# A new written-out instruction order for a linear-attention and MLP-mixer kernel on one core

## The chip, the cores and the metric

The kernel runs on one NeuronCore of a Trainium2 chip. The core has five engines with a queue of instructions each: TensorE (PE, matrix products), VectorE (DVE), ScalarE (ACT), GpSimd (POOL) and SyncE (SP, which here only issues transfers). Each takes its instructions in the order in which the program gives them, and waits at an instruction until what it needs is there. Sixteen DMA engines move data; transfers are issued from SP's or from ACT's queue. The metric is device time in microseconds (us), as the median of several runs.

## The reference

Inputs are q, k, v and alpha of shape (4, 8, 768, 48), that is batch, heads, time, head size, and four weight matrices. First a gated linear recurrence, for every batch and head:

```python
for t in range(S):
    state = alpha[:, :, t, :, None] * state + np.einsum('bhd,bhe->bhde', k[:, :, t], v[:, :, t])
    y[:, :, t] = np.einsum('bhd,bhde->bhe', q[:, :, t], state)
```

Its output, with the heads put side by side, is x of shape (4, 768, 384). Then a mixer:

```python
xt = x.transpose(0, 2, 1)
h = np.maximum(xt @ w_tok1, 0.0) @ w_tok2
u = x + h.transpose(0, 2, 1)
h2 = np.maximum(u @ w_ch1, 0.0) @ w_ch2
return (u + h2).astype(np.float32)
```

w_tok1 is 768 x 256, w_tok2 256 x 768, w_ch1 384 x 1536, w_ch2 1536 x 384. All is float32; the kernel computes its products in bf16 with float32 sums.

## The kernel before

**Blocks.** The recurrence is done in blocks of 256 steps, all 8 heads of a batch at once: 12 blocks, numbered n = 0 to 11, three to a batch. Within a block the decay is split off: the running sum of log alpha gives factors E and IE = 1/E, and with keys times IE and queries times E the block is two ordinary matrix products under a causal mask, plus what the state carries over. A block's operations are named by what they do, with n at the end:

- ld_at, ld_kt, ld_qt, ld_vt (line 545): loads of alpha, k, q, v, 384 KB each, into one of 20 "in" buffers.
- ln, cumw (blocks 0 to 2) or P, ln1, lnP, r1, cum (later blocks): logs on ACT, a pair product P on DVE or POOL, and the running sum as a product on TensorE. E, IE, Et: exponentials on ACT.
- k0a, q0r, kk, kl, qq, ql (lines 645, 649, 653): scaling of keys and queries on DVE or POOL. vb (line 698 or 697): cast of v.
- trk, trq: transposes of keys and queries on TensorE, evk, evq their copies out of the PSUM banks (blocks 0 to 5). From block 6 on the transposes are transfers (dk, dq, line 677) and pq puts the query in order.
- G0_, G1_: the score products of the block's two halves; mask0_, mask1_ (line 720, DVE).
- K: the product of keys and values for the state; vs0_, vs1_, ka, kb, kc are copies that it needs; s, sa, sm bring the state on (DVE or POOL).
- ia, ib: the carried state times queries; y0_, y1_: scores times values, in the same bank; x0_, x1_: the copy of the result.

**Mixer, for each batch b.** t1_b_m_c (line 805): first token product, six steps c (two per block) for m = 0, 1, using the weight pieces wt10 and wt11. ht_b_m: its ReLU. t2_b_i (line 810): second token product, with wt20, wt21, for six row tiles i. u_b_i: the sum with x. up, ut (batches 0, 1) or ux (batches 2, 3, a transfer, line 681): transposes of u. c1_b_m_h (line 829): first channel product for twelve columns m and two halves h, with weight pieces wc10 to wc15 (piece m // 2); rt: its ReLU (ACT line 800 or DVE line 802). c2_b_i_p (line 834): second channel product for row tile i in four parts p, with wc20 to wc25. o_b_i: the sum with u; st_b_i: the store. The last tile (batch 3, i = 0) is cut into 320 columns (h0) and 64 (h1).

**Weights.** 16 pieces of 384 KB are loaded (ldw_, lines 561 to 569) into the same 20 "in" buffers and cast to bf16 on ACT, POOL or DVE (cw_), where they stay.

**What sets the order.** The operations are not emitted in loops: the text ORDER (from line 375) lists all 946 in the order in which they are emitted, each with a letter for its engine: t TensorE, s ACT, v DVE, g POOL, y SP. BUFS lists the buffer that each value takes. An engine's queue is thus the list with only its letter. A load waits until every reader of the buffer's former content is done, and loads on one queue wait in line behind it. Operations marked f (f3_trq0: three, f1_K0: one) are matmuls on zeros that compute nothing and keep TensorE busy; there are 25 such matmuls.

**The shared port.** DVE and POOL operations that only touch SBUF take turns:

```python
        e, last = self.port_turn, self.port_last
        if e:
            if last and last[0] != e:
                self.tc.add_manual_dep(i.ins, last[1].ins.name,
```

So each of them waits for the last one before it in ORDER that ran on the other of the two engines.

Of the kernel before, what the change touches and what calls it, by code (L numbers as in the profile page):

```python
# [892 lines left out]
```

## Time and profile before

| what | value |
|---|---|
| device time, median of 3 runs | 165.01 us (164.99 to 165.9) |
| span of the profiled execution | 163.8 us |
| TensorE busy | 154.4 us (94%) |
| DVE, ACT, POOL busy | 110.7, 101.8, 75.6 us |
| bytes moved | 34.46 MB, mean 210 GB/s |
| issues on SP: inputs and weights, stores, transposes | 52, 16, 16 |
| issues on ACT: inputs and weights, stores | 12, 9 |

The page gives for the profiled execution its span, from the first to the last instruction; its device time is not given apart, so the time that lies around the span is read as the median less the span, 165.0 - 163.8 = 1.2 us. A busy TensorE is not TensorE at its peak, since the ends of its matmuls are modelled. In the stretches, a row is start and end, then the length, the busy time of PE, PE's weight loads, DVE, ACT and POOL with counts, the granted clock of TensorE as a share of full speed, the share of the DMA engines and GB/s. In the order of time, a row is start, length, engine, line, operation, out<-in, shape and count; in brackets the idle time before it and what ended it. In the groups, a row ends with the busy time in all, the mean of one in ns, and the idle time before it.

### The profile page before, as it was taken

What the parts mean: (1) busy time and instruction counts of PE and PEld (TensorE: products, weight loads), DVE (VectorE), ACT (ScalarE), POOL (GpSimd) and SP (SyncE); (2) the same over time, 40 slices, a digit from 0 to 9 for tenths busy, and PEclk for the clock granted to TensorE, in tenths of its full rate; (3) what the DMA queues carried; (4) which work ended last, traced back from release to release, by engine and by line L of the source; (5) the groups of instructions that cost most, each with busy time, mean ns of one, the idle gap of its engine ahead of it and who ended that gap; (6) DMA issues with size and microseconds to landing.
All of it is one profiled execution on the core that took longest, in us unless ns stands there. A gap on an engine that the chain in (4) does not pass through costs nothing.

```text
span 163.8 us, 4061 instructions
## 1 busy us (share of the span) xinstructions
PE 154.4 (94%) x1598; PEld 98.4 (60%) x1598; DVE 110.7 (68%) x197; ACT 101.8 (62%) x188; POOL 75.6 (46%) x94
## 2 busy tenths in 40 slices
PE   7958889899999999999999999999999999999991
PEld 2534656576657666666667666665566566666660
DVE  4244999698799767967889989873591283524341
ACT  3798799998999786389977948465515101562000
POOL 4055489884942827299795384748700000000000
PEclk9987999999999999999999999999999999999999
DMA  5999999999999997996899999689012135220214
GB/s 129 323 319 268 267 343 340 348 341 331 326 372 338 298 299 209 283 310 156 229 254 204 224 127 240 137 216 255 11 48 100 48 71 134 83 100 13 111 71 142
DMA packets 76322, 34.46 MB, mean 210 GB/s; under 512 B 68112, under 2 KB 76304, under 8 KB 76304
## 3 DMA queue, kind: packets, MB, share of 16 engines
q1 hardware_dynamic: 64704, 27.73, 66.2%
q10 hardware_dynamic: 11600, 6.49, 13.1%
q8 instruction: 12, 0.20, 0.5%
q14 instruction: 6, 0.05, 0.1%
HBM read 25.17 MB, written 4.72 MB: 182 GB/s over the span
## 4 chain that ended last, share of the span: by engine, by line
PE 57%; DMA 11%; POOL 9%; DVE 6%; ACT 6%; SPq 5%; issue 3%; ACTq 0%; POOLq 0%
PE ps L834 22%; PE ps L829 21%; DMA in<-in_v_dram 6%; PE ps L604 5%; SPq L545 4%; PE ps L810 4%; DMA in<-in_q_dram 4%; POOL pkk L653 3%; PE ps L805 2%; DMA in<-in_alpha_dram 2%; POOL vb L698 2%; DVE pkk L653 1%; PE ps L821 1%; DVE rt L802 1%; POOL in L645 1%
## 5 line engine op out<-in xcount | busy, mean ns | idle before, releaser
L834 PE MATMUL ps<-wc,rt 128*128 128x384 bf16 (+2 forms) x300 | 54.7, 320 | 0.0
L829 PE MATMUL ps<-ut,wc 128*128 128x384 bf16 x288 | 51.7, 326 | 0.2
L800 ACT ACTIVATE rt<-ps 128x384 bf16<-128x384 f32 x55 | 25.3, 494 | 25.4 <-PE ps L829 23.8
L834 PEld LDWEIGHTS <-rt 128*128 128x128 bf16 x300 | 27.6, 98 | 16.6
L829 PEld LDWEIGHTS <-wc 128*128 128x128 bf16 x288 | 27.1, 98 | 17.3 <-issue 0.7
L802 DVE TENSOR_SCALAR rt<-ps 128x384 bf16<-128x384 f32 x41 | 21.6, 552 | 13.8 <-PE ps L829 13.6
L720 DVE TENSOR_TENSOR gtm<-ps,mk 128x1024 bf16<-128x1024 f32 x24 | 28.3, 1219 | 2.7 <-PE ps L604 2.5
L653 POOL TENSOR_TENSOR pkk<-in,IE 128x384 bf16<-128x384 f32 (+1 forms) x12 | 14.3, 1206 | 9.3 <-DVE pkq L653 5.7
L838 DVE TENSOR_TENSOR o<-ps,u 128x384 f32<-128x384 f32 (+2 forms) x25 | 13.3, 536 | 6.1 <-PE ps L834 6.0
L814 DVE TENSOR_TENSOR u<-ps,x 128x384 bf16<-128x384 f32 x24 | 12.3, 553 | 4.1 <-PE ps L810 4.1
L653 POOL TENSOR_TENSOR pkq<-in,E 128x384 bf16<-128x384 f32 (+1 forms) x8 | 11.2, 1410 | 5.8 <-ACT tpk L697 2.9
L697 ACT CAST x<-ps 128x384 bf16<-128x384 f32 x19 | 9.0, 481 | 7.6 <-PE ps L604 7.6
L697 ACT CAST vb<-in 64x384 bf16<-64x384 f32 (+1 forms) x18 | 11.8, 657 | 2.6 <-POOL vb L698 1.4
L698 POOL CAST vb<-in 64x384 bf16<-64x384 f32 (+1 forms) x17 | 9.5, 559 | 8.0 <-DMA in<-in_v_dram 3.7
L805 PE MATMUL ps<-x,wt 128*128 128x384 bf16 x48 | 11.4, 326 | 0.3 <-ACT x L697 0.3
L810 PE MATMUL ps<-ht,wt 128*128 128x384 bf16 x48 | 10.1, 326 | 0.7 <-ACT wt L697 0.7
L589 POOL TENSOR_TENSOR in<-in 128x384 f32<-128x384 f32 x9 | 9.0, 999 | 3.2 <-DMA in<-in_alpha_dram 2.2
L653 DVE TENSOR_TENSOR pkq<-in,E 128x384 bf16<-128x384 f32 (+1 forms) x9 | 6.0, 689 | 6.3 <-ACT E L637 4.0
L645 POOL TENSOR_TENSOR in<-in,in 128x384 f32<-128x384 f32 x7 | 7.0, 1002 | 5.7 <-DVE in L649 3.0
L604 PE MATMUL ps<-tpq,tpk 48*64 48x128 bf16 (+1 forms) x288 | 8.5, 221 | 1.1 <-DVE ss L762 0.6
L768 DVE TENSOR_TENSOR tmp<-ps,ss 128x384 f32<-128x384 f32 x12 | 6.7, 555 | 4.1 <-POOL ss L771 2.3
L604 PEld LDWEIGHTS <-gtm 128*128 128x128 bf16 x192 | 7.6, 96 | 2.2 <-issue 0.6
(93 smaller groups left out, 212.9 us busy)
## 6 DMA issues: line engine op xcount, KB each, us to landing
in<-in_alpha_dram SPq DMA_DIRECT2D x11, 384.0 KB, 5.9
in<-in_q_dram SPq DMA_DIRECT2D x10, 384.0 KB, 5.5
in<-in_moe_w_ch_dram SPq DMA_DIRECT2D x10, 384.0 KB, 7.4
in<-in_k_dram SPq DMA_DIRECT2D x9, 384.0 KB, 5.3
in<-in_v_dram SPq DMA_DIRECT2D x9, 384.0 KB, 5.3
out_dram<-o SPq DMA_DIRECT2D x14, 192.0 KB, 2.4
out_dram<-o ACTq DMA_DIRECT2D x9, 192.0 KB, 1.9
in<-in_moe_w_tok_dram SPq DMA_DIRECT2D x3, 384.0 KB, 5.5
```

Of the source, the lines that this page charges most:

```text
L604: return self.pe.matmul(out, lhsT=lhsT, rhs=rhs, start=start, stop=stop, skip_group_check=True)
L653: self.shared(self.eng[e].tensor_tensor(self.t(dst)[:, c : c + z, :, 0:D], self.t(src)[:, :, c : c + z, :].rearrange("p h s d -> p s h d") ...
L697: return self.act.copy(d, s)
L698: return self.shared(self.eng[e].tensor_copy(d, s))
L720: self.nc.vector.tensor_tensor(self.t(gtm)[:, hf, :, :], self.pair(gp).rearrange("p a (j t) -> p (a j) t", t=128), bass.AP(tensor=m.tensor ...
L800: self.act.activation(d, s, AF.Relu)
L802: self.nc.vector.tensor_scalar_max(d, s, 0.0)
L805: self.pe.matmul(self.bank(bank)[:, 0:HD], lhsT=self.wt1[:, kc, m * 128 : m * 128 + 128], rhs=self.t(x), start=(kc == 0), stop=(kc == NS - 1))
L810: self.pe.matmul(self.bank(bank)[:, 0:HD], lhsT=self.wt2[:, kc, i * 128 : i * 128 + 128], rhs=self.t(hts[kc]), start=(kc == 0), stop=(kc = ...
L829: self.pe.matmul(self.bank(bank)[:, 0:HD], lhsT=self.wc1[:, kc, mc * 128 : mc * 128 + 128], rhs=self.t(ut)[:, 3 * half : 3 * half + 3, kc, ...
L834: self.pe.matmul(self.bank(bank)[:, 0 : cz - ca], lhsT=self.t(rts[mc][0])[:, i * 128 : i * 128 + 128], rhs=self.wc2[:, mc, ca:cz], start=( ...
L838: self.nc.vector.tensor_tensor(self.t(o)[:, ca:cz], self.bank(bank)[:, 0 : cz - ca], self.t(u)[:, i % 3, ca:cz], ALU.add)
```

## The change

Only ORDER and BUFS differ. The same 946 operations are listed in another order, and some with another letter:

- All loads are issued by SP: twelve that ACT issued before (wt11, wc20, wc25, and loads of blocks 4, 5, 6, 8, 9 and 10) go to SP, 64 in all. Of the stores, 12 go from SP to ACT and 7 from ACT to SP. SP's list has 91 entries instead of 84.
- The first loads are those of batch 0's blocks 0 to 2 and at3, then the four pieces of the token weights (places 14 to 17 among the loads; before: 15, 19, 20, 21), then the channel weights mixed with blocks 3, 4 and 5. kt3, vt3, at4 and qt3, which came ahead of the last token weights, now come after.
- On TensorE, t2 of batch 0 now stands ahead of trk3, cum4, trq3, G_3, K3, ib3 and trk4; 16 instead of 13 fillers stand ahead of cumw0.
- Copies, scalings and ReLUs change engine: 39 from ACT to DVE, 27 from DVE to ACT, 22 from ACT to POOL, 16 from POOL to ACT, 16 from POOL to DVE, 15 from DVE to POOL.
- At the end, the 64-column piece of the last tile comes last instead of the 320-column piece.

```diff
 ORDER = """
-f3_trk0t f1_trq0t f3_trq0t f3_cumw1t f3_cumw0t ld_at0y ln0s ld_at1y ln1s ld_qt0y ld_kt0y ld_vt0y cumw0t E0s ql0v
-ld_at2y f1_K0t f3_K0t cumw1t qq0v trq0t ld_kt1y ld_vt1y IE0s IE1s evq0v ld_qt1y Et0s vb0s kk0g E1s ld_at3y kl0g trk0t
-ln2s Et1s evk0s K0t kk1g kl1g s0_0v cumw2t vb1s vs0_0s Et2s E2s IE2s ld_qt2y vs1_0g qq1v ql1v G0_0t sa1_0t ln13s
-f1_trq1t sm1_0v f3_trq1t G1_0t K1t P3g ld_kt2y ld_vt2y lnP3s trk1t trq1t sa0_1t evk1s evq1s ld_kt3y qq2g mask0_0v
-mask1_0v ldw_wt10y ld_vt3y sm0_1v y0_0t cum3t x0_0s ib0t sa1_1t ld_at4y ld_qt3y ql2v trq2t sm1_1v kl2v E3s IE3s kk2g
-vs0_1g ldw_wt11s y1_0t evq2v G0_1t ia1t kk3g f1_G11t ldw_wt20y ldw_wt21y mask0_1v k0a3g x1_0s G1_1t ld_kt4y vb2s trk2t
-mask1_1v ldw_wc10y ib1t K2t evk2s r13s sa0_2t sm0_2v G0_2t cw_wt10s mask0_2v kl3g ldw_wc11y vs1_1g vs0_2g vs1_2s ka3s
-vb3s f3_G12t G1_2t kb3s ldw_wc13y t1_0_1_0t y0_1t trk3t ld_at5y y1_1t cw_wt11g ib2t ia2t ln14s mask1_2v y0_2t x0_1v
-x0_2v x1_1s vs1_3s vs0_3s ld_qt4s ldw_wc12y kc3g t1_0_1_1t y1_2t t1_0_0_0t t1_0_1_2t P4g t1_0_0_1t t1_0_0_2t t1_0_0_3t
-t1_0_0_4t q0r3g x1_2v t1_0_0_5t t1_0_1_3t evk3v qq3g t1_0_1_4t ql3g lnP4s t1_0_1_5t k0a4g ht_0_0s cw_wt20s K3t ht_0_1v
-cum4t cw_wt21s t2_0_0t t2_0_1t IE4s s0_3v sa1_3v u_0_0v t2_0_2t kk4g ldw_wc15y trq3t u_0_1v u_0_2v t2_0_3t t2_0_5t
-kl4g E4s evq3s up_0_0t t2_0_4t u_0_3v cw_wc10s u_0_5v u_0_4v up_0_1t ut_0_1s ut_0_0v ld_vt4y G1_3t G0_3t up_0_2t ib3t
-mask0_3v mask1_3v trk4t ldw_wc14y c1_0_0_0t c1_0_1_0t cw_wc11g ut_0_2s c1_0_2_0t c1_0_3_1t r14s cw_wc13s ldw_wc21y
-c1_0_7_1t evk4s y1_3t y0_3t rt_0_1_0v q0r4v ka4v qq4v ql4g x0_3s x1_3v rt_0_0_0v rt_0_2_0v P5g cw_wc15g c1_0_7_0t
-c1_0_6_1t rt_0_7_0s rt_0_7_1s cw_wc12s rt_0_3_1s c1_0_0_1t ld_qt5y c1_0_6_0t trq4t c1_0_2_1t c1_0_4_1t ld_kt5y
-ldw_wc22y sm1_3g cw_wc14g vb4g lnP5s c1_0_10_1t evq4s ldw_wc20s rt_0_0_1s rt_0_6_0v rt_0_6_1v ld_vt5s rt_0_2_1s
-c1_0_11_1t c1_0_11_0t rt_0_10_1v cum5t rt_0_11_1v G0_4t G1_4t kb4s IE5s rt_0_4_1v cw_wc21g kc4g ln15s E5s c1_0_10_0t
-c1_0_3_0t r15s rt_0_10_0s c1_0_9_1t vs1_4g ldw_wc23y mask0_4v rt_0_9_1s rt_0_11_0s mask1_4v ldw_wc24y c1_0_8_0t
...
-st_3_2y c2_3_5_1t c2_3_4_1t c2_3_5_2t c2_3_3_1t c2_3_4_2t c2_3_5_3t c2_3_0h0_0t c2_3_4_3t c2_3_3_2t c2_3_0h1_3t o_3_1v
-st_3_1y o_3_5v o_3_4v c2_3_3_3t c2_3_0h0_1t st_3_5y st_3_4y o_3_0h1v st_3_0h1y o_3_3v c2_3_0h0_2t c2_3_0h0_3t o_3_0h0v
-st_3_0h0y st_3_3s
+ld_at0y ln0s f3_cumw1t f3_trq0t f1_K0t f3_trk0t ld_at1y ln1s f3_K0t f3_cumw0t cumw0t Et0s IE0s E0s cumw1t E1s Et1s
+f1_trq1t ld_kt0y kl0g IE1s kk0v trk0t evk0s ld_vt0y vb0g ld_qt0y ld_at2y ln2s f3_trq1t K0t f1_trq0t ql0v qq0v trq0t
+evq0s s0_0v sa1_0t cumw2t G1_0t IE2s ld_qt1y ql1v qq1v trq1t ld_kt1y kk1v mask1_0v sm1_0v kl1g trk1t evk1v ld_kt2y
+vs1_0s E2s ld_vt1y evq1s G0_0t mask0_0v ib0t y1_0t f1_G11t G1_1t mask1_1v vs0_0g vb1s K1t Et2s vs1_1s x1_0s kl2g
+sa0_1t sm0_1v G0_1t mask0_1v ia1t y0_0t x0_0s vs0_1s kk2g trk2t ib1t sa1_1t ld_qt2y qq2g ql2g trq2t evq2s sm1_1v
+ld_vt2y vb2g y0_1t x0_1s ld_at3y ln13s P3g lnP3s K2t sa0_2t f3_G12t evk2v G0_2t G1_2t ia2t vs0_2s sm0_2v ldw_wt10y
+cw_wt10v t1_0_1_0t y1_1t vs1_2g t1_0_0_0t t1_0_0_1t mask0_2v y0_2t t1_0_1_1t t1_0_1_2t ldw_wt11y cw_wt11g x1_1s
+t1_0_1_3t ib2t t1_0_0_2t mask1_2v y1_2t x0_2v t1_0_0_3t ldw_wt21y t1_0_0_4t t1_0_1_4t x1_2s t1_0_1_5t ht_0_1v
+t1_0_0_5t ht_0_0s cum3t E3s IE3s cw_wt21g r13s ldw_wt20y cw_wt20g t2_0_2t t2_0_0t u_0_2v ld_kt3y k0a3g kl3g t2_0_3t
+ldw_wc10y cw_wc10s u_0_0v t2_0_5t t2_0_1t t2_0_4t u_0_3v up_0_1t ut_0_1s u_0_1v up_0_0t kk3g ka3s trk3t u_0_4v u_0_5v
+up_0_2t ut_0_0v c1_0_1_0t ld_at4y P4g c1_0_0_0t kb3g ln14s lnP4s ldw_wc13y cum4t cw_wc13g c1_0_7_0t ldw_wc11y cw_wc11g
+ut_0_2s c1_0_6_1t c1_0_6_0t c1_0_2_0t rt_0_0_0s rt_0_1_0v ld_qt3y qq3v E4s q0r3v ql3v ld_vt3y evk3s ldw_wc14y
+c1_0_3_1t c1_0_3_0t c1_0_1_1t rt_0_6_1v IE4s trq3t vb3g r14s rt_0_6_0v rt_0_3_1s vs0_3g rt_0_7_0s rt_0_2_0s c1_0_7_1t
+ld_kt4y vs1_3s rt_0_3_0s cw_wc14v rt_0_1_1v rt_0_7_1v c1_0_2_1t rt_0_2_1v c1_0_8_0t rt_0_8_0v kc3g K3t c1_0_0_1t evq3s
+G0_3t ldw_wc15y s0_3v cw_wc15s G1_3t c1_0_8_1t rt_0_8_1s kk4g k0a4g kl4g kb4s sa1_3v ld_at5y P5g ld_qt4y qq4g
+c1_0_10_0t q0r4g c1_0_11_1t mask1_3v ib3t mask0_3v c1_0_11_0t y1_3t c1_0_9_0t y0_3t rt_0_0_1v trk4t ldw_wc12y
+rt_0_10_0s rt_0_11_1v lnP5s cum5t x0_3v rt_0_11_0s cw_wc12s c1_0_5_0t c1_0_4_1t ldw_wc21y ldw_wc20y ql4v trq4t evk4v
+c1_0_5_1t x1_3v rt_0_9_0s rt_0_4_1v ln15s cw_wc21s c1_0_4_0t rt_0_4_0v rt_0_5_0v c1_0_10_1t cw_wc20g c2_0_4_0t evq4s
+G1_4t rt_0_10_1s sm1_3g ldw_wc22y cw_wc22v rt_0_5_1s G0_4t mask0_4v ia4t c2_0_1_0t c2_0_4_1t c2_0_1_1t ld_vt4y
+ldw_wc24y vb4s vs0_4s E5s r15s ldw_wc23y cw_wc23s y0_4t x0_4s c2_0_0_0t c2_0_2_0t ka4v cw_wc24s ld_at6y ln16s mask1_4v
+kc4g vs1_4g K4t P6v c1_0_9_1t sa0_4v sm0_4v sa1_4v c2_0_0_1t lnP6s c2_0_2_1t rt_0_9_1s IE5s r16s c2_0_4_2t ld_qt5y
+q0r5v cum6t c2_0_1_2t ib4t c2_0_0_2t ld_kt5y qq5v trq5t k0a5v kk5v c2_0_2_2t ldw_wc25y cw_wc25v evq5s y1_4t x1_4s
+ld_vt5y vb5g trk5t evk5v c2_0_4_3t IE6s c2_0_1_3t o_0_1v ld_at7y E6s sm1_4g o_0_4v t1_1_1_0t t1_1_1_1t t1_1_1_2t ln17s
+G0_5t G1_5t ld_kt7y mask1_5v k0a7g c2_0_0_3t c2_0_2_3t mask0_5v vs1_5s c2_0_5_0t c2_0_5_1t P7g vs0_5s kc5s K5t sa0_5v
+sm0_5v c2_0_5_2t ia5t y0_5t c2_0_5_3t ib5t ld_vt6y y1_5t ld_kt6y k0a6v t1_1_0_0t t1_1_0_1t t1_1_1_3t t1_1_0_2t kk6v
+ld_at9y ld_qt6y o_0_0v t1_1_0_3t x0_5s x1_5s t1_1_1_4t t1_1_1_5t ht_1_1v ld_vt7y vb6g lnP7s t1_1_0_4t t1_1_0_5t
+ht_1_0s vs0_6g ld_at8y c2_0_3_0t o_0_5v cum7t E7s IE7s t2_1_3t u_1_3v t2_1_5t u_1_5v st_0_1s q0r6g t2_1_1t c2_0_3_1t
...
+c2_3_1_2t o_3_4v c2_3_2_1t c2_3_1_3t c2_3_3_1t c2_3_3_2t c2_3_3_3t o_3_3v st_3_3y o_3_1v st_3_1y st_3_4s c2_3_5_3t
+o_3_5v st_3_5s c2_3_2_2t c2_3_2_3t o_3_2v c2_3_0h0_1t c2_3_0h0_2t c2_3_0h0_3t c2_3_0h1_0t c2_3_0h1_1t c2_3_0h1_2t
+o_3_0h0v st_3_0h0s c2_3_0h1_3t o_3_0h1v st_3_0h1s st_3_2y
...
 """
 BUFS = """
-3 0 4 1 11 1 13 0 5 3 11 2 0 0 1 6 0 1 2 0 0 17 0 0 9 1 0 1 2 0 1 0 1 16 0 4 0 2 0 6 0 4 7 1 3 3 1 6 1 0 5 2 1 6 5 2 1
...
+9 0 1 0 4 3 18 1 6 1 1 2 0 6 13 0 1 0 1 4 2 1 0 1 0 2 0 1 0 5 1 12 0 0 2 7 0 14 15 0 4 1 6 1 0 4 2 2 3 2 0 6 0 7 1 19
...
 """
```

More of the change, by code (lines that the diff above doesn't have):

```diff
@@ new lines @@
+c1_1_11_0t K6t o_0_2v c1_1_2_0t c1_1_2_1t IE8s ln18s k0a8v qq7v r18s s0_6v sa1_6v rt_1_2_1v rt_1_2_0v c1_1_10_0t
+c1_1_3_1t rt_1_3_1v c1_1_1_1t rt_1_1_1s c1_1_6_0t c1_1_4_1t rt_1_4_1v P9g c1_1_5_0t lnP9s ld_vt8y ld_qt9y c1_1_7_1t
+kk8g rt_1_7_0v rt_1_10_0s c1_1_5_1t sm1_6g kb7s ka7s ld_qt8y c1_1_8_1t rt_1_6_0s cum9t rt_1_7_1s q0r9g vs1_7g
+rt_1_5_0s c1_1_8_0t vb8v rt_1_0_1v st_0_2y rt_1_8_0v kc7s c1_1_6_1t vs0_8g rt_1_8_1v c2_1_1_0t rt_1_6_1v IE9s
+rt_1_11_0s K7t c1_1_3_0t rt_1_3_0v q0r8g dq6y pq6s ld_kt9y c1_1_9_0t qq8g rt_1_5_1s dq7y sa0_7v sm0_7v c1_1_10_1t
@@ new lines @@
+ia10t qq11g u_2_2v u_2_0v ux_2_0y y0_9t o_1_5v G0_10t c2_1_2_3t mask0_10v ld_kt11y c1_2_7_1t IE11s c1_2_4_1t rt_2_4_1s
+o_1_0v x0_9v y0_10t c1_2_9_1t st_1_0y c1_2_11_1t c1_2_1_1t rt_2_1_1v x0_10v rt_2_7_1s c1_2_0_1t c1_2_6_0t o_1_2v
+st_1_2s c1_2_10_1t rt_2_11_1s k0a11g c1_2_8_0t kk11g c1_2_6_1t c1_2_2_1t t1_3_0_0t rt_2_2_1s rt_2_10_1v rt_2_8_0s
+rt_2_6_0v st_1_5y dq11y c1_2_5_1t rt_2_0_1v c1_2_1_0t rt_2_1_0s ld_vt11y st_1_1y c1_2_0_0t c1_2_3_1t rt_2_5_1v
+rt_2_9_1s K10t c1_2_3_0t dk11y rt_2_6_1s rt_2_3_0s c1_2_8_1t c1_2_10_0t t1_3_0_1t t1_3_0_2t rt_2_0_0s sa0_10v
```

71 lines of the change are left out of this document (26 added, 45 removed), and 20 rows, old and new, of the table BUFS.

## The prediction

> **What bounds the kernel now.** I read the page's slices first, then the stretches (start:end in us, busy time of each engine, granted clock, DMA share, GB/s), then TensorE's own order of time.
>
> ```profile
> span 163.8 us, 4061 instructions
> PE   7958889899999999999999999999999999999991
> 20.00:36.00 16.00, 14.37 (x215) 10.12 (x213) 14.66 (x23) 15.51 (x27) 14.09 (x17) 1.00 1.12 342
> 36.00:56.00 20.00, 19.86 (x207) 13.12 (x205) 17.23 (x29) 17.86 (x35) 10.95 (x15) 1.00 1.10 338
> 56.00:100.00 44.00, 44.00 (x515) 28.70 (x514) 36.93 (x62) 33.17 (x65) 30.38 (x31) 1.00 1.05 231
> 100.00:160.50 60.50, 60.15 (x504) 37.19 (x502) 31.32 (x56) 20.87 (x44) 11.80 (x14) 1.00 0.41 108
> ```
>
> From 36 to 160.5 us TensorE idles for 0.14 + 0.00 + 0.35 us in all. So the end is set by the moment from which TensorE is full, by the work still ahead of it then, and by new holes. The amount of work is the same in both orders (393 PE entries, 25 fillers). The question is only what happens before 36 us and whether holes open later.
>
> ```profile
> 1.06 4.51 PE L604 MATMUL ps<-zs 128*128 128x512 bf16 x13 [1.06 <-DVE zs L507]
> 5.41 0.65 PE L604 MATMUL ps<-la,u 128*128 128x384 bf16 x3
> 6.29 1.02 PE L604 MATMUL ps<-zs 128*128 128x512 bf16 x4
> 10.50 0.62 PE L666 MATMUL ps<-idn,pkk 128*128 128x128 bf16 x8 [1.71 <-POOL pkk L653]
> 29.40 0.33 PE L604 MATMUL ps<-vb,pkk 128*128 128x96 bf16 x4
> 29.57 0.33 PE L604 MATMUL ps<-vb,kt 128*128 128x96 bf16 x4
> 29.95 0.32 PE L604 MATMUL ps<-la,u 128*128 128x384 bf16 x1
> 31.05 1.15 PE L810 MATMUL ps<-ht,wt 128*128 128x384 bf16 x6 [0.67 <-ACT wt L697]
> 32.04 0.62 PE L666 MATMUL ps<-idn,pkq 128*128 128x128 bf16 x8
> 32.50 0.81 PE L810 MATMUL ps<-ht,wt 128*128 128x384 bf16 x4
> 34.24 0.62 PE L604 MATMUL ps<-tpq,tpk 48*128 48x128 bf16 x16
> 34.79 0.51 PE L821 MATMUL ps<-idn,u 128*128 128x128 bf16 x6
> 35.46 0.62 PE L666 MATMUL ps<-idn,pkk 128*128 128x128 bf16 x8
> 35.92 2.60 PE L829 MATMUL ps<-ut,wc 128*128 128x384 bf16 x15
> ```
>
> The second token product (t2) starts at 31.05, after 0.67 us of waiting for the cast of a token weight, the first channel product (c1) at 35.92. From there on TensorE is full.
>
> **The change, part by part.** *Loads.* When does the k-th load land? Three waits on a landing show it:
>
> ```profile
> 4.31 0.84 ACT L598 ACTIVATE la<-in 128x768 bf16<-128x768 f32 x1 [2.23 <-DMA in<-in_alpha_dram]
> 16.63 0.52 ACT L592 ACTIVATE lf<-in 128x384 f32<-128x384 f32 x1 [0.44 <-DMA in<-in_alpha_dram]
> 32.48 1.00 POOL L645 TENSOR_TENSOR in<-in,in 128x384 f32<-128x384 f32 x1 [0.50 <-DMA in<-in_k_dram]
> ```
>
> These are the 1st, 10th and 22nd load, so from the 10th on (32.48 - 16.63)/12 = 1.32 us each. In the new list wt20, the last of the token weights, is 17th, where before the last of them was 21st: an estimated 25.9. kt3 is 18th: 27.2.
>
> *The start of attention.* 16 fillers now stand ahead of cumw0 instead of 13, at 0.215 us (four from 6.29 to 7.15): cumw0 starts at 6.05, not 5.41. Then a chain, with these rows:
>
> ```profile
> L631 ACT ACTIVATE E<-ps 128x400 f32<-128x400 f32 x9 | 4.5, 504 | 0.1
> L637 ACT ACTIVATE IE<-ps 128x768 f32<-128x768 f32 x3 | 2.4, 811 | 0.2 <-PE ps L604 0.2
> 12.08 1.95 POOL L653 TENSOR_TENSOR pkk<-in,IE 128x384 bf16<-128x384 f32 x2 [1.63 <-DMA in<-in_k_dram]
> L698 POOL CAST wc<-in 128x768 bf16<-128x768 f32 x6 | 5.0, 825 | 0.2
> 7.31 1.03 DVE L653 TENSOR_TENSOR pkq<-in,E 128x384 bf16<-128x384 f32 x2 [3.97 <-ACT E L637]
> 19.12 1.31 ACT L697 COPY tpq<-ps 128x1024 bf16<-128x1024 bf16 x1
> 16.03 2.35 DVE L720 TENSOR_TENSOR gtm<-ps,mk 128x1024 bf16<-128x1024 f32 x2
> 18.30 0.55 DVE L762 TENSOR_TENSOR ss<-ps,E 128x384 bf16<-128x384 f32 x1
> 28.00 0.69 DVE L698 COPY tpk<-ps 128x1024 bf16<-128x1024 bf16 x1
> ```
>
> cumw0 takes 0.9 (5.41 to 6.29), IE0 0.8 after a short Et0: 8.15. DVE and POOL take turns at their shared port in the written order, so kl0 (POOL 1.0), kk0 (DVE 0.55), vb0 (POOL 0.83) and ql0, qq0 (DVE 1.03) add up, then trq0 0.5, evq0 1.3, G1_0 0.35 and handoffs of about 0.4: the first mask starts at 14.1. From it to x0_2 DVE does six masks at 1.13, four state products at 0.47, two key copies at 0.69, one weight cast at 0.55, one x at 0.5: 11.1 us. With 0.7 for waits between x0_2 is done at 25.9. x1_2, the last t1, ht and IE3 follow on ACT and PE (0.5 each): IE3 at 28.2.
>
> The clock can lengthen this:
>
> ```profile
> 11.00:12.00 1.00, 1.00 (x20) 0.74 (x18) 0.02 (x1) 1.00 (x3) 0.00 (x0) 0.51 1.17 325
> 13.00:14.00 1.00, 1.00 (x19) 0.72 (x18) 0.00 (x0) 0.79 (x1) 1.00 (x2) 0.50 1.04 285
> ```
>
> Before, TensorE idled from 8.8 to 10.5 (the 1.71 above) and then had half its clock from 11 to about 14. The new order has holes of 1.1 and 0.7 us at 7.8 and 9.1 (waiting for E0, then kk0), so both are possible. At half clock trk0, three fillers, K0, trq0 and cumw2 cost 1.1 us more: IE3 28.2 to 29.4. [...]
>
> *t2 and c1.* t2 can start at about 27.4 (wt20 landed and cast, ht done). New is that trk3, whose input is made by three POOL products k0a3, kl3, kk3 of 1.0 us, stands on TensorE ahead of the first c1. k0a3 starts with kt3 at 27.2, kl3 with IE3 at 28.2 to 29.4, kk3 ends at 30.3 to 31.4, trk3 (0.46) and one up (0.34) follow: c1 at 31.2 to 32.3; I take 31.8, 4.1 us earlier than before.
>
> Against it stands work that before did ahead of c1 and the new order leaves for later: K3 0.34 (29.40 to 29.57, twice), cum4 0.29, trq3 0.46 (32.04 to 32.50), G0_3 and G1_3 0.55 (34.24 to 34.79), ib3 0.17 (four like K3's), trk4 0.46 (35.46 to 35.92). Sum 2.27. What is left is 1.8 us.
>
> *New waits after c1.* c1_0_7_0 needs the cast of wc13, which on POOL stands behind kk3, P4 (1.0) and kb3 (0.5): 30.85 + 1.0 + 0.5 + 0.83 = 33.2, and TensorE is there at 31.8 + 0.98 (two c1, six matmuls at 0.163) + 0.29 (cum4) = 33.07: 0.2 with the handoff. wc13's load must also wait until wt20's cast frees their common buffer; its issue at 27.4 and a landing 4 to 4.7 us later come before POOL is free. c1_0_9_1 gets its bank from x0_4, now behind the cast of wc23 on ACT: 0.45. pq9 moved from POOL to ACT behind x1_8, 0.2 ahead of G1_9. Together 0.9; bounds 0 and 1.5. Of the first c2 (wc20, 32nd load, 45.7 by the pace, cast 46.5; TensorE comes there at about 46.9) nothing is charged.
>
> *What costs nothing.* Twelve loads go from ACT's queue to SP's.
>
> ```profile
> 26.88 0.39 ACTq L545 DMA_DIRECT2D in<-in_q_dram  x1
> 26.87 0.51 ACT L697 COPY kt<-pkk 64x384 bf16<-64x384 bf16 x1
> 67.76 4.14 SPq L677 DMA_TRANSPOSE tpk<-pkk  x1
> 160.52 0.49 DVE L838 TENSOR_TENSOR o<-ps,u 128x320 f32<-128x320 f32 x1 [0.66 <-PE ps L834]
> ```
>
> An issue on ACT lay beside its compute, so ACT gains nothing. On SP the later ones (kt8, vt8, vt9, kt10) now stand behind transposes that hold SP for up to 4.14 us. By the same walk kk8 is wanted on POOL at about 74 us and vb8 at 78, some 8 us after those issues: covered; without the cover a wait there goes straight into K8 on TensorE. The evictions and scalings that change engines (ACT to DVE 39, DVE to ACT 27, and so on) lie under a full TensorE after 36 us; DVE there has 2.8 of 20 us free, ACT 2.1. They are priced only where named above.
>
> *The end.* The last add is over 64 columns instead of 320 (0.49), but the 320-column one now ends just before it: between 0 and 0.3, I take 0.2, nearer the row that stays.
>
> Sum: 4.1 - 2.27 - 0.9 + 0.2 = 1.1 us earlier. The execution profiled has a span of 163.8; the times shown have a median of 165.01, 1.2 above it, which I take as unchanged: 165.0 - 1.1 = **163.9**.
>
> **The rivals.**
>
> *TensorE is never held after t2* (the POOL chain is ready in time). t2 at 27.4, then t2 2.0 (twelve matmuls at 0.163), up 1.0 (three at 0.34, 34.79 to 35.13 as one stands there), trk3 0.46: c1 at 30.9; 5.0 - 2.27 + 0.2 gives 162.1. For it: POOL is idle for 1.9 of the 16 us here. Against it: kk3 alone needs 3 us after kt3.
>
> *One queue delivers more slowly, and the channel weights come late.* This ends slower.
>
> ```profile
> 3.00:12.00 9.00, 7.29 (x72) 4.19 (x71) 2.68 (x7) 6.80 (x11) 1.96 (x2) 0.95 1.16 322
> 12.00:20.00 8.00, 6.77 (x93) 4.31 (x92) 5.74 (x10) 6.30 (x10) 4.45 (x5) 0.85 1.01 266
> ```
>
> With loads from SP alone the rate was 322 GB/s, then 266; with both queues in use 342 and 338 (first fence). At 266 a load of 393 KB takes 1.48 us. The place is c2_0_4_3, which needs wc25, the 40th load: 16.63 + 30 x 1.48 = 61.0, cast 61.6, against a TensorE that comes there at about 57.5: 4.1 us idle, 168.0. It decides from 1.32 us a load (298 GB/s) and makes the kernel 1% slower from 1.41 (279 GB/s). Buffer waits push the same way: wc13 waits for wt20's cast, wc12 for wc14's, wc24 for wc12's, vt5 for wc24's, and all behind them on SP wait too, where ACT's queue went around. Against it: the 322. [...]
>
> *The clock stays halved for a second stretch:* another 1.1 us ahead of IE3: 165.0.
>
> *The change doesn't do what it says:* the weights land earlier, but the port chain of DVE and POOL, not the weights, holds t1 and t2. For it: only 0.67 us before t2 are put down to the weight. With ht at 29.5 instead of 27, c1 comes at 33.9: 2.0 - 2.27 - 0.9 + 0.2, that is 166.0.
>
> **How the numbers follow.** Forecast 163.9 (162.9 to 165.0 by its bounds): 0.43. TensorE never held, 162.1: 0.14. Slow queue, 165.5 to 168.5: 0.26. Clock, 165.0: 0.07. Port chain, 166.0: 0.10. About 1% (1.65 us) is what a measurement tells from no change. Faster by over 1% (below 163.4): the second case and 0.12 of the first, 0.26. Slower by over 1% (above 166.7): 0.25 of the slow queue and 0.03 of the last, 0.28. Within 1%: 0.46. The range runs from 162.2 to 168.0 and leaves out the fastest of the second case and the slowest of the third.
>
> **What would show it.** Right: the first L810 near 27.4, the first L829 between 31.2 and 32.3 with a wait for POOL pkk ahead of trk3, and a TensorE without holes above 0.5 us from 34 on. The slow queue shows as a rate under 300 GB/s from 20 to 56 us and TensorE waiting for the cast of a channel weight. The port chain shows as t2 starting at 29 or later on a wait for ht. The forecast is wrong if holes open after 60 us, in blocks 6 to 11, for which I found 0.8 to 2 us of slack and no more.

## The result, and the profile after

The changed kernel takes **171.49 us** (median of 4 runs, 169.44 to 171.8); the kernel before took 165.31 us beside it on the same chip (4 runs, 164.99 to 165.9). The ratio is 1.033, with a 95% interval of 1.025 to 1.040: slower by 3.3% (6.2 us between the medians). Here and below, an execution that is over 1.5% above the fastest of its kernel counts as slow and is left out of the medians and the ratios. The prediction said 163.9 us, with 162.2 to 168.0 as its range, so it was wrong, and on the wrong side; none of its rivals reached this time either (the slowest of them ended at 168.5). The profiled execution of the changed kernel took 171.42 us with a span of 169.7 us.

First the slices of the page, the line to set beside that of before:

```profile
span 169.7 us, 4034 instructions
...
PE   7977999899999999987989879997999999999992
```

The front is as full as it was before. The new dips stand in the 18th to the 28th slice, between about 72 and 119 us, where the kernel before had none. In the same four stretches of both kernels (start:end, busy time of PE, PEld, DVE, ACT, POOL, granted clock, DMA share, GB/s), first the kernel before:

```profile
20.00:35.00 15.00, 13.37 (x200) 9.26 (x198) 13.66 (x23) 14.51 (x26) 13.21 (x16) 1.00 1.11 342
35.00:60.00 25.00, 24.86 (x274) 16.80 (x272) 21.36 (x35) 22.27 (x43) 13.68 (x18) 1.00 1.10 330
60.00:80.00 20.00, 20.00 (x159) 12.72 (x156) 15.55 (x31) 14.97 (x30) 14.31 (x16) 1.00 0.93 231
80.00:100.00 20.00, 20.00 (x309) 13.15 (x308) 18.24 (x27) 14.79 (x28) 14.23 (x13) 1.00 1.16 218
```

and the changed kernel:

```profile
20.00:35.00 15.00, 13.75 (x163) 8.89 (x161) 11.00 (x19) 11.98 (x23) 11.21 (x14) 1.00 1.06 321
35.00:60.00 25.00, 24.63 (x266) 15.81 (x265) 22.92 (x39) 21.43 (x40) 11.98 (x16) 1.00 1.03 297
60.00:80.00 20.00, 18.17 (x156) 11.33 (x155) 15.74 (x28) 12.55 (x28) 11.80 (x11) 1.00 1.12 259
80.00:100.00 20.00, 18.14 (x252) 11.63 (x251) 15.10 (x24) 16.13 (x32) 15.74 (x15) 1.00 1.03 210
```

TensorE is idle for 1.83 us from 60 to 80 and 1.86 us from 80 to 100, where before it was idle for nothing. One more difference is easy to pass over: from 35 to 60 us the DMAs move 297 GB/s instead of 330, and VectorE is busy for 22.92 of 25 us instead of 21.36.

What TensorE waits for (its order of time, the rows from 60 us on with a wait of 0.27 us or more):

```profile
76.01 1.14 PE L829 MATMUL ps<-ut,wc 128*128 128x384 bf16 x6 [0.64 <-DVE o L838]
77.81 1.34 PE L829 MATMUL ps<-ut,wc 128*128 128x384 bf16 x6 [0.67 <-DVE ss L762]
79.43 3.09 PE L829 MATMUL ps<-ut,wc 128*128 128x384 bf16 x18 [0.28 <-DVE rt L802]
87.96 0.42 PE L604 MATMUL ps<-tpq,tpk 48*64 48x128 bf16 x15 [0.52 <-DVE tmp L768]
98.48 1.14 PE L834 MATMUL ps<-wc,rt 128*128 128x384 bf16 x6 [1.34 <-DVE o L838]
100.75 0.37 PE L604 MATMUL ps<-vb,gtm 128*128 128x48 bf16 x8 [0.27 <-DVE gtm L720]
116.72 1.62 PE L829 MATMUL ps<-ut,wc 128*128 128x384 bf16 x9 [1.03 <-ACT rt L800]
```

Mostly it waits for VectorE, and twice for the add that writes an output tile (L838). That add is short (0.56 us); so what does VectorE itself wait for? Its waits from 55 to 125 us, the largest group (total, times, longest):

```profile
DVE o L838 <- DMA out_dram<-o: 4.7, 2, 2.4
```

and the two instructions in its order of time:

```profile
75.40 0.56 DVE L838 TENSOR_TENSOR o<-ps,u 128x384 f32<-128x384 f32 x1 [2.41 <-DMA out_dram<-o]
...
97.87 0.56 DVE L838 TENSOR_TENSOR o<-ps,u 128x384 f32<-128x384 f32 x1 [2.33 <-DMA out_dram<-o]
```

There are four output buffers. Tile 0_2 at 75.40 takes the buffer of tile 0_0, and tile 1_3 at 97.87 that of tile 0_5. Both old tiles had been added long ago (near 65 and 66 us), but their stores were issued late, by ScalarE (its first four stores, start and length of the issue; ACTq and SPq are the issuing sides of ScalarE and SP):

```profile
66.12 0.37 ACTq L585 DMA_DIRECT2D out_dram<-o  x1
70.65 0.34 ACTq L585 DMA_DIRECT2D out_dram<-o  x1
86.60 0.34 ACTq L585 DMA_DIRECT2D out_dram<-o  x1
94.28 0.34 ACTq L585 DMA_DIRECT2D out_dram<-o  x1
```

The second row is the store of 0_0, the fourth that of 0_5. While VectorE stands 2.4 us for such a landing, its evictions of PSUM banks stand behind it, and TensorE finds no bank (its waits of 0.64 and 1.34 us for L838 above). This is what is put to the test below. In the trace no instruction that VectorE has behind either add starts before it: the next ones start at 75.87 and 98.34.

To see where time goes in executions of different orders, I counted for each the work that TensorE has begun by a given moment. Each piece counts with the time that it takes in the trace of before when nothing holds it (the median: 0.49 us for a piece of a channel product, 0.16 for a step of the first token product), 142.9 us in all without the fillers, the same for every kernel here. The table shows how far each profiled execution is ahead (+) of the kernel before, in us, at seven moments from the start of its span:

```
at us                            35    65    70    80    90   100   130
changed kernel                 +1.2  +0.1  +0.1  -2.4  -3.1  -4.7  -6.1
two stores earlier             +1.8  +0.4  +0.4  -1.3  -2.0  -2.0  -3.0
four stores earlier            +0.7  -1.1  -1.1  -2.4  -3.1  -3.1  -4.2
twelve loads back on ScalarE   -3.7 -11.9 -12.3 -13.9 -15.2 -18.1 -28.0
new front, old rest            +2.1  -0.5  -1.3  -5.9  -5.8  -5.7  -6.3
four more steps moved          +1.7  +0.5  -0.3  -2.5  -2.7  -4.3  -4.8
two stores, second queue       +0.8  -0.7  -0.7  -1.1  -1.8  -1.9  -3.5
four stores, second queue      +2.1  -1.0  -1.0  -1.4  -2.2  -2.2  -2.4
before, loads on SP            -1.6  -1.6  -1.6  -2.7  -2.5  -2.5  -2.6
before, SP, two DMAs back      +0.2  -0.8  -1.4  -3.2  -3.1  -3.1  -3.3
before, SP, two places         -0.5  -1.0  -1.0  -1.0  -1.0  -1.0  -0.4
before, one store              +0.3  -0.1  -0.1  -4.2  -4.1  -4.1  -3.7
```

The changed kernel is 1.2 us ahead at 35 us, has lost nearly all of that by 65 us without one large hole, and then falls 6.1 us behind: 2.5 between 70 and 80, 2.3 from 80 to 100, the rest up to 130. One execution says little about tenths: the first eight rows, all but the fourth, have the same order up to 35 us and differ by 1.4 us there. The verdicts below go by the medians.

### The profile page after: what moved, and what is told of

Read it like the earlier page. It is cut to its first block, busy times and chain, and to the rows that moved or that the text cites. A ratio compares the mean times of both kernels' runs of the same rounds, so it can differ in the third digit from the quotient of the medians.

```text
span 169.7 us, 4034 instructions
## 1 busy us (share of the span) xinstructions
PE 156.3 (92%) x1598; PEld 97.8 (58%) x1598; DVE 115.9 (68%) x210; ACT 98.2 (58%) x182; POOL 74.2 (44%) x87
## 5 line engine op out<-in xcount | busy, mean ns | idle before, releaser
L829 PE MATMUL ps<-ut,wc 128*128 128x384 bf16 x288 | 51.8, 326 | 3.2 <-ACT rt L800 1.0
L829 PEld LDWEIGHTS <-wc 128*128 128x128 bf16 x288 | 27.0, 97 | 20.9 <-issue 4.0
L800 ACT ACTIVATE rt<-ps 128x384 bf16<-128x384 f32 x48 | 21.8, 487 | 28.9 <-PE ps L829 26.0
L802 DVE TENSOR_SCALAR rt<-ps 128x384 bf16<-128x384 f32 x48 | 24.5, 551 | 9.1 <-PE ps L829 9.0
L838 DVE TENSOR_TENSOR o<-ps,u 128x384 f32<-128x384 f32 (+2 forms) x25 | 13.0, 537 | 17.8 <-PE ps L834 13.0
L653 POOL TENSOR_TENSOR pkk<-in,IE 128x384 bf16<-128x384 f32 (+1 forms) x13 | 17.0, 1314 | 9.8 <-ACT IE L637 5.7
L697 ACT CAST x<-ps 128x384 bf16<-128x384 f32 x16 | 7.5, 478 | 14.9 <-PE ps L604 7.1
L653 POOL TENSOR_TENSOR pkq<-in,E 128x768 bf16<-128x768 f32 (+1 forms) x8 | 12.0, 1509 | 1.4 <-DVE ss L771 0.7
L604 PE MATMUL ps<-zs 128*128 128x512 bf16 x25 | 8.3, 473 | 1.9 <-DVE zs L507 1.1
L810 PE MATMUL ps<-ht,wt 128*128 128x384 bf16 x48 | 9.4, 326 | 0.3 <-ACT ht L800 0.3
L589 POOL TENSOR_TENSOR in<-in 128x384 f32<-128x384 f32 x8 | 8.0, 999 | 3.8 <-DVE pkq L653 3.8
L771 POOL TENSOR_TENSOR ss<-tmp,E 128x384 bf16<-128x384 f32 x7 | 5.8, 834 | 7.8 <-DVE tmp L768 7.7
L604 PE MATMUL ps<-vb,gtm 128*128 128x48 bf16 x192 | 8.7, 184 | 0.5 <-DVE gtm L720 0.5
L697 ACT COPY tpq<-ps 128x1024 bf16<-128x1024 bf16 x6 | 7.8, 1308 | 2.2 <-PE ps L666 2.0
```

Source lines behind the costliest of these rows:

```text
L604: return self.pe.matmul(out, lhsT=lhsT, rhs=rhs, start=start, stop=stop, skip_group_check=True)
L653: self.shared(self.eng[e].tensor_tensor(self.t(dst)[:, c : c + z, :, 0:D], self.t(src)[:, :, c : c + z, :].rearrange("p h s d -> p s h d") ...
L697: return self.act.copy(d, s)
L800: self.act.activation(d, s, AF.Relu)
L802: self.nc.vector.tensor_scalar_max(d, s, 0.0)
L810: self.pe.matmul(self.bank(bank)[:, 0:HD], lhsT=self.wt2[:, kc, i * 128 : i * 128 + 128], rhs=self.t(hts[kc]), start=(kc == 0), stop=(kc = ...
```

## The experiments

All times are medians of up to four executions; the kernel before, beside them, was at 165.5 to 165.8. My theory at first: the late stores. The rivals: all loads in SP's one queue, and the new order being late in many small places.

### Two stores earlier

```diff
- ... u_1_5v st_0_1s q0r6g ... c1_1_0_0t st_0_0s kb6s ... c2_1_1_3t st_0_5s y0_6t
+ ... u_1_5v st_0_1s st_0_5s st_0_0s q0r6g ... c1_1_0_0t kb6s ... c2_1_1_3t y0_6t
```

> The changed kernel with two of its stores issued earlier: ScalarE issues the stores of output tiles 0_0 and 0_5 right behind that of 0_1, near 66.5 us, and not at 70.65 and 94.28; nothing else is touched. Late stores (my theory): VectorE's two waits for an output buffer, 2.41 us at 75.4 and 2.33 us at 97.87, are gone, and with them TensorE's idle time of about 1.8 us between 70 and 80 and 1.6 us between 95 and 101: about 168 us, from 171.5. One queue (rival): the loads that all stand on SP are what is late, VectorE waits for them instead: 171 to 172 us. New order as a whole (rival: scalings and copies on other engines, late at many small places): 170 to 171.5 us, with the idle time moved and not gone.

Measured: 168.44 us (167.62 to 169.31), ratio 1.019 (1.012 to 1.026). The distance to before falls from 6.2 to 2.9 us. The tile's view of the outputs shows what their adds still wait for:

```profile
its engine sat idle before it (us, times) until:
  PE ps L834: 13.0, 7
```

The 4.7 us of waiting for a store are gone, and nothing takes their place there. Late stores are the larger half of the loss. But it is half: the single queue or the order must have the rest.

### Four stores earlier

```diff
  (the run with two stores earlier; | parts separate places)
- dk7y rt_1_4_0s | q0r11g st_0_3y E11s | o_1_2v st_1_2s c1_2_10_1t rt_2_11_1s ... rt_2_2_1s
+ dk7y st_0_3y rt_1_4_0s | q0r11g E11s | o_1_2v c1_2_10_1t rt_2_11_1s ... rt_2_2_1s st_1_2s
```

> The same as the run with two earlier stores, and two more moved: the store of 0_3 is issued by SP behind the transpose of block 7's keys (near 72 us) and not between the two transposes of u at 107.8; the store of 1_2, on which ScalarE waited 2.71 us for VectorE, stands two relus later on ScalarE. Late stores: another 1 to 1.5 us (TensorE's wait of 1.03 us for ScalarE's relu at 116.7, and 1.3 us of SP ahead of the second transpose of u): about 167 us. One queue: 171 to 172 us. New order as a whole: 169 to 171 us.

Measured: 167.44 us (167.06 to 169.46), ratio 1.015 (1.008 to 1.023). The median is 1.0 us lower, as expected, though the intervals overlap. The wait of 1.03 us at 116.7 is gone from TensorE's list. What is left there is another:

```profile
109.35 0.34 PE L604 MATMUL ps<-ss,tpq 128*128 128x96 bf16 x4 [1.18 <-POOL tpq L698]
```

This is the last reorder of block 10's queries, which the change moved to GpSimd. (The profiled execution took 169.46 us, 2.0 above the median, and came out of the front 0.5 us later than that of the changed kernel.)

### The twelve loads back on ScalarE

```diff
- ldw_wt11y ... ld_qt4y ... ldw_wc20y ... ld_kt10y      (twelve loads, places unchanged)
+ ldw_wt11s ... ld_qt4s ... ldw_wc20s ... ld_kt10s
```

> The changed kernel with the twelve loads that ScalarE issued before (token weight 1, channel weights 2 of 0 and 5, eight tiles of blocks 4 to 10) issued by ScalarE again, at their new places; stores untouched. One queue: at least 2 us faster, 169.5 or less. Late stores: within 1 us of 171.5, both waits for an output buffer still there; slower if ScalarE, which works in order, stands at a load whose input buffer is not free.

Measured: 199.4 us, ratio 1.21. Neither theory's number; only the addition "slower if ScalarE stands" pointed this way. The table has 3.7 us lost by 35 us and 12 by 65: at these places ScalarE reaches each load only after whatever it computes first, so the weights come late from the start (token weight 1 is issued at 21.9 and lands at 29.0; in the changed kernel it is issued at 18.3 and lands at 24.2). The letters without the places cost 27.9 us here; the run tells the two theories apart only in that the single queue is no loss that letters alone undo.

### The kernel before, with all loads on SP

```diff
- ldw_wt11s ... ld_qt4s ... ldw_wc20s ... ld_kt10s      (the same twelve, in the order of before)
+ ldw_wt11y ... ld_qt4y ... ldw_wc20y ... ld_kt10y
```

> The kernel before with those twelve loads issued by SP, at their old places, and nothing else. One queue: it pays here too, 167.5 us or more, from 165.3. Late stores: within 1 us of 165.3, because the stores of the kernel before follow their tiles.

Measured: 168.0 us (167.95 to 168.08), ratio 1.016 (1.012 to 1.021). The single queue alone costs 2.5 us in the order of before: the rival is right as well. The rows that carry it, two of TensorE, one of VectorE, and SP's issues around the store in question:

```profile
29.17 1.15 PE L805 MATMUL ps<-x,wt 128*128 128x384 bf16 x6 [1.52 <-POOL wt L698]
...
75.50 0.65 PE L829 MATMUL ps<-ut,wc 128*128 128x384 bf16 x3 [0.88 <-DVE o L838]
...
74.89 0.56 DVE L838 TENSOR_TENSOR o<-ps,u 128x384 f32<-128x384 f32 x1 [1.62 <-DMA out_dram<-o]
...
68.80 0.51 SPq L545 DMA_DIRECT2D in<-in_v_dram  x1
69.36 0.58 SPq L545 DMA_DIRECT2D in<-in_k_dram  x1
70.38 0.41 SPq L585 DMA_DIRECT2D out_dram<-o  x1
```

A token weight comes late, and then the same thing as in the changed kernel: the store of tile 0_5 now stands behind two loads on SP, is issued at 70.38 instead of 66.61, and VectorE waits for its buffer. The queue does part of its harm through a store.

### New front, old rest

```diff
  order and engines of the changed kernel up to o_0_5v
- ... its rest
+ ... what is left, in the order and on the engines of before; buffers of this part chosen anew
```

> The changed kernel's order and engines up to output tile 0_5 (near 66 us, all loads by SP until there), and from there the order and engines of the kernel before, its loads on ScalarE and its stores included; buffers of the second part chosen anew. By the starts of TensorE's instructions in the two traces, the work that the changed kernel has done is 1.2 us ahead of before at 35 us, 0.0 us ahead at 65 us, and 6.2 us behind at 130 us. If the loss is all behind 66 us (my theory, the stores and the other late steps of the new second part): 165 to 165.8 us, as before. If the front keeps its lead and only the profiled run lost it: 164 us. If the front leaves the second part its loads and buffers late (rival): 167 us or more, with TensorE idle between 70 and 120 though the old order stands there.

Measured: 169.16 us (168.92 and 169.4), ratio 1.022 (1.013 to 1.031). My theory's 165 to 165.8 fell; the rival, that the front leaves the second part its loads late, gave 167 or more, with idle time from 70 on, and that is what came. ScalarE's order of time:

```profile
66.70 0.43 ACTq L545 DMA_DIRECT2D in<-in_alpha_dram  x1
...
72.70 0.52 ACT L592 ACTIVATE lf<-in 128x384 f32<-128x384 f32 x1 [3.99 <-DMA in<-in_alpha_dram]
```

and TensorE's row behind it:

```profile
75.74 3.33 PE L829 MATMUL ps<-ut,wc 128*128 128x384 bf16 x12 [2.38 <-ACT ut L697]
```

Before, block 10's decays were issued at 61.94. This trace is of an execution of 171.78 us: behind the hole of 2.38 us TensorE has half its clock from 76.46 to 79.88, and the two executions behind the median, whose mean clock is 1.00, had no such stretch. So the rows show the place of the hold and not its usual size. By the issue rows, the kernel before has issued 40 of its 64 loads by 45 us and the changed one 35; at 80 us it is 57 against 55. (The run isn't a clean cut: buffers are chosen anew, and the load that holds here belongs to the second part, where ScalarE issues it 4.8 us later than before. What it shows is that the old rest does not keep its time behind the new front.)

### The kernel before, all loads on SP but one, and a store on ScalarE

```diff
  (the kernel before with all loads on SP)
- ldw_wt11y ... st_0_5y
+ ldw_wt11s ... st_0_5s
```

> The kernel before with ten of the twelve loads issued by SP, and two DMAs on ScalarE at their old places: the load of token weight 1 (its cast held TensorE 1.68 us at 27.25 with all twelve on SP, 0.50 us before) and the store of output tile 0_5 (it stood behind loads on SP, and VectorE waited 1.62 us at 74.89 for its buffer). If the single queue costs only through what stands behind it in order (my theory): 165.5 to 166.2 us, from 168.0. If the transfers themselves are slower in one queue (rival): 167.3 to 168 us, and the loads' median from issue to landing is longer than the 5 to 6 us of before.

Measured: 167.95 us (166.48 to 168.77), ratio 1.012 (1.003 to 1.020). (This is with eleven of the twelve loads on SP; the expectation counts ten.) The number is the rival's, but its sign is missing: by kind of load, the medians from issue to landing are 4.9 to 6.5 us on SP, 4.1 to 7.4 before. The weight's part came as my theory had it (TensorE waits 0.34 us at 28.1, for a copy of x as before, and not 1.52 us for the weight). The store's did not: on ScalarE it was issued at 71.09, later than on SP, because a cast ahead of it waited 2.75 us for a load, and VectorE then waited 2.40 us for its landing. I had moved it from one queue to a worse one. Two later runs, each with the store at one place, separate the two.

### Four stores earlier and four more steps moved

```diff
  (the run with four stores earlier)
- qq8g ... sm0_7v | pq10g | dk6y ld_qt7y ... ld_kt8y | rt_1_4_0s ... rt_1_11_1s ... lnP8s
+ sm0_7v qq8g | ka10s pq10s | ld_qt7y ld_kt8y dk6y | lnP8s rt_1_4_0s ... rt_1_11_1s
```

> The run with four earlier stores, and four more steps moved, each of which held TensorE in its trace: the scaling of block 8's queries (GpSimd) behind the state product of block 7 (0.80 us at 87.6); the last reorder of block 10's queries on ScalarE and not on GpSimd (1.34 us at 108.1); the loads of block 7's queries and block 8's keys ahead of the transpose of block 6's keys (0.97 us between 77 and 79); block 8's logarithm of the product ahead of two relus (0.44 us at 74.4). If late single steps are the whole loss (my theory): the sum of the four is 3.5 us, most of it kept, 164.5 to 166 us. If the new order is late everywhere (rival), other waits take their place: 166.5 to 167.5 us.

Measured: 170.33 us (169.07 to 170.61), ratio 1.027 (1.021 to 1.034): slower than the run it started from, and beyond the rival's number too. Each hold that I took away came back elsewhere; TensorE's two largest now:

```profile
75.92 0.34 PE L604 MATMUL ps<-vb,pkk 128*128 128x96 bf16 x4 [1.33 <-POOL pkk L698]
93.55 0.33 PE L604 MATMUL ps<-ss,tpq 128*128 128x96 bf16 x4 [1.21 <-ACT x L697]
```

With two loads ahead of it, SP issues the transpose of block 6's keys 3 us later (69.3, from 66.4), and GpSimd may overwrite those keys only after it; that is the first row. Moving a step by its own wait, without what stands behind it, is what went wrong here, as in the prediction.

### A second queue for five loads

```diff
- ld_vt4y, ld_qt5y, ld_at6y, ld_kt6y, ld_qt7y                    (at their places)
+ rt_0_2_0s ld_vt4s | cw_wc15s ld_qt5s | rt_0_9_0s ld_at6s | vb4s ld_kt6s | vs1_5s ld_qt7s
```

> The run with two earlier stores, and five loads issued by ScalarE at places that it passes early and whose input buffers are free by then: block 4's values (near 36.7 us, from 42 on SP), block 5's queries (39.5, from 46), block 6's decays (44, from 46) and keys (48.5, from 57), block 7's queries (59, from 66). From 35 to 60 us the loads ran at 330 GB/s before, and at 290 to 301 in every run in which SP issues them all. If SP, which stands still whenever the next load's buffer is not free, holds the rate down (my theory): 315 GB/s or more there, TensorE's waits between 70 and 80 us (1.8 us in that run) are halved, 166.5 to 167.5 us, from 168.4. If the rate is that of the transfers (rival): 300 GB/s or less, 168 to 169 us.

Measured: 169.12 us (168.22 to 169.92), ratio 1.020 (1.014 to 1.026).

> The same five loads on ScalarE in the run with four earlier stores. SP holds the rate down: 315 GB/s or more from 35 to 60 us, 165.8 to 166.8 us, from 167.4. The rate is that of the transfers: 167 to 168 us.

Measured: 167.51 us (167.12 to 168.74), ratio 1.012 (1.005 to 1.019). So no gain in either. The stretch of 35 to 60 us, in the run with two stores earlier, then with five loads on ScalarE added to it:

```profile
35.00:60.00 25.00, 24.48 (x264) 15.66 (x262) 22.67 (x38) 21.57 (x41) 12.91 (x17) 1.00 1.02 290
```

```profile
35.00:60.00 25.00, 24.59 (x256) 15.61 (x255) 22.60 (x39) 21.23 (x40) 11.89 (x16) 1.00 1.06 317
```

The rate rises as my theory said, 290 to 317, and by the table the loss from 70 to 80 us falls from 1.7 to 0.4. The other run has 303. But the time does not follow: half of the theory holds, its price does not. In the second run the reason shows: loads that go ahead push the channel weights back (ScalarE, then TensorE; without the five loads the two waits are 0.39 and 0.29 us).

```profile
52.44 0.83 ACT L697 CAST wc<-in 128x768 bf16<-128x768 f32 x1 [1.26 <-DMA in<-in_moe_w_ch_dram]
53.70 0.65 PE L829 MATMUL ps<-ut,wc 128*128 128x384 bf16 x3 [0.87 <-ACT x L697]
```

For the first run no such row stands out, and its profiled execution left the front 1.0 us later than the one it is compared with, in code that is the same. Where its gain went stays open.

### The kernel before, one store on another engine

```diff
- st_0_5y
+ st_0_5s
```

> The kernel before with one edit: the store of output tile 0_5 is issued by ScalarE at its old place in the order, and not by SP. ScalarE gets there near 70.5 us (SP: 66.5), and tile 0_3, which takes the same buffer, was due on VectorE at 71.5. If a store's place on its engine decides (my theory): VectorE waits 1 to 4 us for the store's landing, TensorE 0.5 to 2 us for PSUM banks, 166.0 to 167.5 us, from 165.5. If the engine that issues a store is free of cost, as the prediction had it (rival): within 0.5 of 165.5.

Measured: **169.25 us** (168.85 to 170.07), ratio 1.022 (1.016 to 1.028). One letter, 3.6 us. The chain in three rows (ScalarE's issue, VectorE, TensorE):

```profile
69.80 0.40 ACTq L585 DMA_DIRECT2D out_dram<-o  x1
...
74.98 0.56 DVE L838 TENSOR_TENSOR o<-ps,u 128x384 f32<-128x384 f32 x1 [3.16 <-DMA out_dram<-o]
...
75.59 1.12 PE L829 MATMUL ps<-ut,wc 128*128 128x384 bf16 x3 [2.42 <-DVE o L838]
```

The store is issued 3.2 us later than in the kernel before, it lands 5 us on, and tile 0_3, due at 71.6, starts at 74.98. The table has nothing else: even at 70 us, 4 us behind at 80, and so to the end. It is more than I expected, because the hole itself is not all: behind it TensorE's granted clock falls to half, from 75.48 to 78.89 us. In the stretch from 76 to 78:

```profile
76.00:78.00 2.00, 2.00 (x14) 1.24 (x13) 1.40 (x3) 1.23 (x3) 0.64 (x2) 0.50 0.79 138
```

The hole of 2.42 us and 3.41 us at half clock, some 1.7 us of work, make the 4.1 us of the table. The kernel before has a clock of 1.00 there. It is no matter of this execution alone: the mean clock is 0.98 in each one that counts here, and 0.987 or more in the kernel before beside them.

### The kernel before, all loads on SP but one, the store moved up

```diff
  (the kernel before with all loads on SP)
- ldw_wt11y ... dk6y u_1_4v ld_vt8y ld_kt8y ... st_0_5y
+ ldw_wt11s ... dk6y st_0_5y u_1_4v ld_vt8y ld_kt8y ...
```

> The kernel before with eleven of the twelve loads issued by SP (168.0 us with all twelve); token weight 1 is loaded by ScalarE as before, and the store of output tile 0_5 stays on SP but stands ahead of block 8's two loads, right behind the transpose of block 6's keys, near 68.7 us and not 70.3. If the single queue costs through the two steps that stood behind it (my theory): the hold of 1.68 us at 27.25 is 0.5 us as before, VectorE's wait of 1.62 us for the output buffer is under 0.3 us, 165.5 to 166.4 us. If loads in one queue are late everywhere (rival): 167.2 to 168 us, with other waits in their place between 60 and 80 us.

Measured: 166.22 us (165.88 to 167.33), beside 165.81 before, ratio 1.010 (1.000 to 1.020). The median lies in my range; the interval alone does not exclude the rival's 167.2. In the profiled execution (165.88) the waits are as I expected: 0.34 us at 28.1 as before, none for a store, and no hold of TensorE from 47 to 120 us. Two steps carry most of what the single queue costs in this order; how much of the 2.5 us is left is within the scatter of these runs and is not settled.

## Why the prediction was wrong

**The front was right.** The first L810 and the first L829 in the changed kernel, and GpSimd's kl3 and kk3:

```profile
27.73 2.11 PE L810 MATMUL ps<-ht,wt 128*128 128x384 bf16 x12 [0.31 <-ACT ht L800]
31.65 1.14 PE L829 MATMUL ps<-ut,wc 128*128 128x384 bf16 x6
33.47 2.77 PE L829 MATMUL ps<-ut,wc 128*128 128x384 bf16 x16 [0.41 <-POOL wc L698]
29.05 1.96 POOL L653 TENSOR_TENSOR pkk<-in,IE 128x384 bf16<-128x384 f32 x2
```

27.73 against 27.4, 31.65 against 31.8, and the wait for GpSimd's cast of a channel weight 0.41 instead of 0.2. GpSimd's chain ends at 31.01, inside the forecast's 30.3 to 31.4. The wait for it ahead of trk3, which I had named as a sign, is small all the same: TensorE stands some 0.25 us, in the middle of trk3, because t2 started 0.3 us later than forecast and another 0.25 went ahead of up. The clock stayed at 1.00, so the second stretch at half speed, one of the rivals, did not come. Of 4.1 us earlier less 2.27 us of work left for later and 0.2 of waiting, 1.6 should be left at 35 us; the table has 1.2 in this execution, and 0.7 to 2.1 in others with the same front. The rival "port chain" (t2 at 29 or later) fell with these rows; "never held after t2" (c1 at 30.9) missed too, though by no more than these small waits.

**The step that failed is "What costs nothing".** It has three parts.

The stores are missing from it. Nineteen of them change their engine, and the sum has a term for waits after c1 (0.9) without any for an output buffer: I never asked, for each output tile, whose buffer it takes and when that store is issued. By the starts of its instructions TensorE lost 2.3 us between 74 and 80 and 2.1 between 96 and 101, the stretches of those two waits; 3.3 us (6.2 to 2.9 above before) came back when only these two stores were moved; one store moved in the kernel before costs 3.6 us by itself, some 1.7 of them by the half clock behind its hole. In the changed kernel no hole was followed by half a clock: the granted clock is 1.00 up to 168.84 us, past the end of TensorE's last instruction (166.57). A third store, on which ScalarE stood 2.71 us, held TensorE 1.03 us at 116.7.

The loads on SP were priced at nothing with a cover of some 8 us. The rival "one queue delivers more slowly" named the sign to look for, a rate under 300 GB/s from 20 to 56 us. Over that stretch it was 307 (323 to 36 us, 295 from there), against 339 before, so the sign came in part. (By the rival's own numbers, cast at 61.6 for a landing at 61.0, it decides from 1.34 us a load, 293 GB/s, and not from 1.32.) Its place was wrong: no channel weight holds TensorE in the changed kernel after 34 us. What is late are the loads of blocks 6 to 10 (kt6 is issued at 57.4 and not 51.1, at10 at 81.9 and not 61.9), and the stores that stand among them. In the order of before the single queue alone costs 2.5 us; what it costs in the new order no run shows cleanly. The landings show no slower queue (in the medians 4.8 to 6.2 us by kind of load here, 4.1 to 7.4 before), but the rate differs: from 35 to 60 us it is 290 to 309 GB/s in six runs in which SP issues all loads of that time (297 in the changed kernel), 330 and 329 in the order of before with the twelve on ScalarE. SP stands still where the next load has to wait for something (its waits from 20 to 60 us add up to 13.8 us in the changed kernel, and to 18.7 in the kernel before, where ScalarE issued loads beside it); the rise from 290 to 317 with five loads on ScalarE fits that, but brought no time.

The scalings and evictions were said to lie under a full TensorE, with 2.8 of 20 us free on VectorE. From 35 to 60 us it now has 2.1 of 25 free (3.6 before), and from 35 to 65 us TensorE loses the lead of the front again: by the starts of its instructions in nine delays of 0.1 to 0.4 us, 1.7 in all (before: three, 0.6 in all). That VectorE's load is the reason is argued from these numbers and not shown; no run took it away.

**What I said would make it wrong** is what happened: holes after 60 us, in blocks 6 to 9. I had put it at the end as a condition, with "0.8 to 2 us of slack", and given it no rival and no price of its own; output buffers, where the holes came from, are not named in it. The tail behaved as forecast: the work is 6.1 us behind at 130 us, and the span 5.9 us longer.

What stays open: about 2 us of the loss (four stores earlier is still at 167.4) is spread over late loads and moved steps. Each attempt to take it away by single moves brought it back elsewhere, and no version here beats the kernel before.

## What to carry to other kernels

Two stores came onto the critical path here because their buffers had a next user: VectorE stood 2.41 and 2.33 us for them, and TensorE lost 2.3 and 2.1. So for every ring of buffers list who takes the buffer over, when the store before it is issued (behind what, on its own engine), and add its landing, 1.9 to 5.0 us here. In a kernel whose TensorE is full, a new order is not judged by its front alone; the lead of 1.2 us here was smaller than what one late buffer cost. And where several engines issue DMAs, ask what stands ahead of one on the engine that it goes to: by its letter alone the store of tile 0_5 was issued 3.2 us later.
